# Attention with a gated MLP on one core: k and v loads of later heads moved, the last burst reordered, its last pieces stored from where they are made

## The chip, the cores and the metric

One core of one Trainium2 chip. The metric is the device time of one execution in microseconds (us), as a median over executions. Most questions here are about one or two microseconds in 544, so each result comes with the range of its executions, and comparisons use ratios with a 95% interval. A profiled execution is one of these; its span (first to last instruction) is some 1.8 us shorter than its device time.

All outputs are right.

## The reference, cut to what matters

```python
xn = layernorm(x)                              # x: 2048 x 448
q = (xn @ wq)                                  # 16 heads of 256
k, v = k_cache[last 512], v_cache[last 512]    # 8 heads, each used by two q heads
s = (softmax(q @ k.T / 16) @ v) @ wo           # 2048 x 448
g = silu((gelu(xn @ w_gate) * (xn @ w_up)) @ w_down)
return x + s * g
```

## The kernel before

The kernel is one static program: operations are listed in order, and semaphore waits follow from the buffers that they read and write. The first 145 us make the layer norm and the gates g. The gates go to DRAM (`g_all`) and come back in tiles. Then 64 "heads" follow: 4 chunks of 512 queries by 16 heads. For a head, `s_mm` makes scores and exponentials p; two DMA transposes (`pT<-pn`) turn p for four tiles; `pv`, two heads later (LAG), multiplies by v. Every eight heads a query group makes q for the next eight. After each chunk, a "burst" multiplies o with wo: seven products of halves and sums in place of eight (a Strassen-like scheme), combined on VectorE (DVE).

k and v of the 8 key heads are loaded partly late, because their room is used by temporaries of the gates before. The places of the temporaries of the last two chunks of gates are set here:

```python
a_v, a_th = b_va[3].lo, at2 + 3 * TD
dn[2] = places(2, [(2, a_v), (1, a_v + SD), (0, b_pT[2][0].lo)],
               [a_v + 2 * SD, b_pT[2][0].lo, b_pT[2][0].lo + CD], [a_th])
dn[3] = places(3, [], [a_v + 2 * SD, a_v + SD, a_v + SD + CD], [a_th])
```

The loads stand in the main loop, between the query pairs of the group at head 4 (m == Q0) and the group at head 12 (m == Q0 + QS); `gates3` computes the last gates and stores them:

```python
if m == Q0 and p < 3:
    K.reuse(b_kT[2:6] + b_va[3:4] if p == 0 else b_kT[6:] + b_va[4:] if p == 2 else [])
    for k in ((2, 3, 4, 5), (), (6,))[p]:
        load_k(k)
    if p == 0:
        load_v(3)
    if p < 2:
        gates3(2 * p)
        gates3(2 * p + 1)
    else:
        load_v(4)
        load_v(5)
        K.reuse([b for y in b_xr for b in y])
        for t in range(NG2):
            load_g2(t)
        for t in range(NXR):
            dma("pool", xr[:, t, :], x_view[:, t, :], (), b_xr[t])
if m == Q0 + QS and p == 0:
    load_k(7)
    load_v(6)
    load_v(7)
```

The loads of g and x at the end of that stretch are issued by GpSimd and feed the first burst, over 70 us later. `load_g2(t)` reads `g_all`, so it waits for the gates' stores.

In the burst, B1 is the bank (in the last burst: two banks, one for each half of 128 rows) of the first product, B6, B7, B5, B3 those of the products with sums, B4 that of product 3:

```python
def product(j, b, lhs, hs, first, reads, ts=(0, 1)):
    mms([(bank[b][:, t * N2:(t + 1) * N2], lhs(h)[:, t * P:(t + 1) * P], wt[:, WAT[j], h, :],
          first and h == hs[0] and t == ts[0], False) for h in hs for t in ts],
        reads + [b_wt[j][i] for i in sorted({h * NB // Hq for h in hs})], (b_ps[b],))

def first_two(j, hs, first):
    A1 = A(j, 0)
    for ts in (((0,), (1,)) if last else ((0, 1),)):
        product(j, B1[ts[0]], A1, hs, first, bA(j, hs), ts)
```

```python
for n in range(3):
    sums(n)
first_two(0, allh[:Hq - LAG], True)
if last:
    pv(late.pop(0))
    pv(late.pop(0))
first_two(0, allh[Hq - LAG:], False)
if last:
    K.reuse(b_lastt + b_lastg)
    for i in range(2):
        dma("pool", lastt[:, i, :], g2d[NT - 2 + i], (b_g2d[NT - 2 + i],), (b_lastg[i],))
    dma("pool", lastt[:, 2, :], x_view[:, NT - 1, :], (), b_lastt)
    for t in range(2):
        cs = slice(t * N2, (t + 1) * N2)
        act(U2[:, cs], bank[B1[t]][:, cs], ACT.Copy, (b_ps[B1[t]],), bU2, scale=F)
else:
    act(U2, bank[B1[0]][:, 0:D], ACT.Copy, (b_ps[B1[0]],), bU2, scale=F)
    product(3, B4, A(1, 1), allh, True, bA(1, allh))
for n in range(Hq // HB):
    hs = allh[n * HB:(n + 1) * HB]
    for j, i, b in ((5, 2, B6), (6, 3, B7), (4, 0, B5), (2, 1, B3)):
        product(j, b, lambda h, n=n, i=i: sr[n % 3][:, i, h % HB, :], hs, n == 0, [b_sr[n % 3][i]])
    if n == 0:
        sums(3)
if last:
    product(3, B4, A(1, 1), allh, True, bA(1, allh))
first_two(1, allh, False)
plus(U2, bU2, B6, U2, bU2)
plus(U3, bU3, B7, U2, bU2)
if not last:
    part(1, 0, B4, U3, bU3)
part(1, 1, B5, U3, bU3)
plus(U2, bU2, B5, U2, bU2)
part(0, 1, B3, U2, bU2)
ends((2, 1), (3, 1), (0, 1), (1, 1))
if last:
    part(1, 0, B4, U3, bU3)
    ends((2, 0), (3, 0))
for t in range(2):
    first_part(t)
    ends((t, 0))
```

After the last matmul, `first_part` copies half a bank to SBUF on ScalarE (ACT), and `burst_end` multiplies by g, adds x and stores:

```python
def burst_end(t, ns=(0, 1)):

    t4 = t % 4
    x, bx = (xr[:, t % NXR, :], b_xr[t % NXR]) if t < NT - 1 else (lastt[:, 2, :], b_lastt)
    g, bg = (g2[:, t % NG2, :], b_g2[t % NG2]) if t < NT - 2 else (lastt[:, t % 2, :], b_lastg[t % 2])
    cs = slice(ns[0] * N2, ns[-1] * N2 + N2)
    bx, by = [[b[n] for n in ns] for b in (bx, b_xs[t4])]
    add("dve", xs[:, t4, cs], xs[:, t4, cs], g[:, cs], by + [bg], by, ALU.mult)
    if t + NG2 < NT - 2:
        load_g2(t + NG2)
    add("dve", x[:, cs], xs[:, t4, cs], x[:, cs], by + bx, bx)
    dma("sp" if t >= NT - 4 else "pool", out_view[:, t, cs], x[:, cs], bx, ())
    if t + NXR < NT - 1:
        dma("pool", xr[:, t % NXR, :], x_view[:, t + NXR, :], (), b_xr[t % NXR])
```

The softmax here doesn't subtract the row's maximum and nothing guards it: scores larger than these inputs give would overflow.

## Time and profile before

| | before |
|---|---|
| device time, 3 runs | 543.7 us median (543.29 to 545.11) |
| profiled span | 542.4 us |
| TensorE busy | 536.5 us, 99% |
| TensorE waits after the start | head 4's p (pT) 0.9 us, o of the last chunk (oTh) 0.3 us |
| from the last ACT copy's start to the end | 3.23 us |

How to read the lines in this document. In the list of waits, a line says which engine at which source line waited for what, the sum in us, how often, and the longest. In a timeline, a line gives start, duration, engine, source line, operation, output<-input, shapes, how many instructions it lumps together, and in brackets the idle time before it and what ended it. SPq and POOLq are the queues of the SyncE and GpSimd engines as issuers of DMA. The source line is nearly always that of a helper (one line for all matmuls, one for all copies on ACT, and so on), so tiles tell the operations apart: pT<-pn the transposes of p, g<-g_all and xr<-in_A_x_dram the GpSimd loads, bank<-kT,qT scores, bank<-pT,va p times v, bank<-wt,oTh and bank<-wt,sr the products of the burst.

The *lost start* before a matmul is the distance between its start and the start of the one before, less that one's columns / 2.4 ns and 2.5 ns. The *landing* of a DMA is the moment when the last of its 16 parts has counted its semaphore up.

### The profile page before, as it was taken

The page shows a single profiled execution, that of the slowest core. Times are in us where ns is not written, and L with a number is a line of the kernel's source. Part 1 is how long each engine was busy: PE and PEld are TensorE (multiplying, and loading weights), DVE is VectorE, ACT ScalarE, POOL GpSimd, SP SyncE. Part 2 cuts the span into 40 slices and gives each one's busy share as a digit, 9 for nine tenths or more (in the row PEclk, how much of TensorE's full clock was granted, in tenths as well). Part 3 has the DMA queues.
Part 4 walks back from the last instruction along what each step waited for, and adds up shares of the span by engine and source line. Part 5 has one row for each costly group of instructions (what it writes and reads, how often), then busy time and mean ns, then how long its engine had stood idle before and what let it go on. Part 6 is the DMA issues. An engine that isn't in the chain of part 4 may idle for free.

```text
span 542.4 us, 10788 instructions
## 1 busy us (share of the span) xinstructions
PE 536.5 (99%) x4106; PEld 305.8 (56%) x4106; DVE 375.8 (69%) x823; ACT 313.8 (58%) x784; POOL 39.6 (7%) x78
## 2 busy tenths in 40 slices
PE   8999999999999999999999999999999999999997
PEld 5554457449644444984444469544444984444487
DVE  6673885799767757934875786367568934776875
ACT  5433854873667858216875860488488116877720
POOL 1130400000001000003001000120100003001010
PEclk9999999999999999999999999999999999999999
DMA  9569261931499848302781670076457502863621
GB/s 292 125 184 132 47 140 42 272 92 43 114 194 190 156 113 149 70 1 70 166 152 47 153 139 1 18 150 146 94 102 156 64 1 78 160 151 85 155 48 34
DMA packets 171459, 61.36 MB, mean 113 GB/s; under 512 B 154960, under 2 KB 168272, under 8 KB 171408
## 3 DMA queue, kind: packets, MB, share of 16 engines
q1 hardware_dynamic: 167632, 51.39, 45.0%
q0 software_dynamic: 3008, 8.72, 6.7%
q8 instruction: 32, 0.52, 0.4%
q10 hardware_dynamic: 768, 0.57, 0.3%
q14 instruction: 19, 0.16, 0.1%
HBM read 19.76 MB, written 3.67 MB: 43 GB/s over the span
## 4 chain that ended last, share of the span: by engine, by line
PE 93%; ACT 2%; DVE 2%; DMA 2%; issue 1%; ACTq 0%
PE bank L391 92%; ACT p L843 2%; DMA pT<-pn 2%; DVE pn L850 1%; PE bank L508 1%; DVE rden L847 0%; ACT qT L382 0%; PE bank L489 0%; ACT oTh L382 0%; ACT xnT L382 0%; DVE xnT L385 0%; DVE xr L385 0%; DVE gl L421 0%; DVE epst L422 0%; ACTq L155 0%
## 5 line engine op out<-in xcount | busy, mean ns | idle before, releaser
L843 ACT ACTIVATE p<-bank 128x512 f32<-128x512 f32 x256 | 150.5, 596 | 28.8 <-DVE pn L850 26.0
L391 PE MATMUL bank<-pT,va 128*128 128x512 bf16 x512 | 120.9, 379 | 1.0 <-DMA pT<-pn 0.9
L391 PE MATMUL bank<-kT,qT 128*128 128x512 bf16 x512 | 121.0, 379 | 0.0
L850 DVE TENSOR_SCALAR pn<-p,rden 128x512 bf16<-128x512 f32 x256 | 113.1, 484 | 10.2 <-DMA pT<-pn 6.0
L391 PE MATMUL bank<-xnT,wq 64*128 64x512 bf16 x768 | 94.9, 376 | 0.0
L391 PEld LDWEIGHTS bank<-pT,va 128*128 128x128 bf16 x512 | 49.7, 98 | 62.0 <-DMA pT<-pn 3.4
L391 PEld LDWEIGHTS bank<-kT,qT 128*128 128x128 bf16 x512 | 49.4, 98 | 61.7 <-issue 3.4
L391 PE MATMUL bank<-xnT,wgu 64*128 64x512 bf16 (+2 forms) x768 | 83.8, 350 | 0.2
L382 ACT ACTIVATE qT<-bank 128x512 bf16<-128x512 f32 x76 | 44.1, 596 | 51.7 <-PE bank L391 50.1
L828 DVE CAST qT<-bank 128x512 bf16<-128x512 f32 x52 | 34.9, 690 | 49.6 <-PE bank L391 49.6
L391 PEld LDWEIGHTS bank<-xnT,wq 64*128 64x128 bf16 x768 | 36.7, 94 | 46.3 <-ACT p L843 2.1
L391 PEld LDWEIGHTS bank<-xnT,wgu 64*128 64x128 bf16 x768 | 36.8, 94 | 37.2 <-issue 0.6
L847 DVE RECIPROCAL rden<-rsum 128x2 f32<-128x2 f32 x128 | 21.2, 165 | 46.0 <-ACT p L843 45.8
L843 ACT ACTIVATION_READ_ACCUMULATOR p<-bank 128x1 f32 x256 | 51.6, 202 | 0.0
L391 PE MATMUL bank<-wt,sr 128*128 128x224 f16 x512 | 49.7, 259 | 0.0
L382 ACT ACTIVATE gl<-bank 128x512 bf16<-128x512 f32 x56 | 33.1, 596 | 28.5 <-PE bank L391 26.1
L391 PEld LDWEIGHTS bank<-wt,sr 128*128 128x128 f16 x512 | 49.1, 98 | 0.0
L382 ACT ACTIVATE xnT<-bank 128x224 bf16<-128x224 f32 (+2 forms) x12 | 4.4, 398 | 71.6 <-PE bank L391 70.9
L868 DVE TENSOR_SCALAR oTh<-bank 128x512 f16<-128x512 f32 x62 | 42.4, 684 | 0.0
L382 ACT ACTIVATE oTh<-bank 128x512 f16<-128x512 f32 x66 | 38.9, 589 | 4.7 <-PE bank L391 4.7
L391 PE MATMUL bank<-wt,oTh 128*128 128x224 f16 x384 | 38.3, 259 | 0.3 <-ACT oTh L382 0.3
L391 PEld LDWEIGHTS bank<-wt,oTh 128*128 128x128 f16 x384 | 36.7, 98 | 1.8 <-ACT oTh L382 1.1
(80 smaller groups left out, 408.2 us busy)
## 6 DMA issues: line engine op xcount, KB each, us to landing
wtb<-in_A_wo_dram POOLq DMA_DIRECT2D x4, 896.0 KB, 10.9
wq<-in_A_wq_dram SPq DMA_DIRECT2D x2, 1536.0 KB, 7.9
va<-in_A_v_cache_dram SPq DMA_DIRECT2D x8, 256.0 KB, 3.9
pT<-pn SPq DMA_TRANSPOSE x128, 2.8
xr<-in_A_x_dram POOLq DMA_DIRECT2D x15, 112.0 KB, 2.3
wd<-in_B_w_down_dram SPq DMA_DIRECT2D x1, 1568.0 KB, 8.5
g<-g_all POOLq DMA_DIRECT2D x14, 112.0 KB, 2.3
out_dram<-xr POOLq DMA_DIRECT2D x12, 112.0 KB, 2.1
```

Of the source, the lines that this page charges most:

```text
L382: K.op("act", lambda e, o=o, i=i: e.activation(o, i, func, scale=scale), reads, writes)
L391: ins = e.matmul(o, lhsT=l, rhs=r, start=st, stop=sp, skip_group_check=True)
L508: ins = e.matmul(bank[b][:, 0:w], lhsT=gl[:, 0, 0:P], rhs=gl[:, 0, 0:w], start=True, stop=True)
L828: K.op("dve", lambda v, s=s, b=b: v.tensor_copy(qT[:, s, 1, :], bank[b + 1]), (b_ps[b + 1],), (b_qT[s][1],))
L843: K.op("act", lambda e, b=b, r=r, z=z: e.activation(p32[:, z, :], bank[b], ACT.Exp, scale=att_scale, accum_out=rsum[:, r:r + 1]), (b_ps[b] ...
L847: K.op("dve", lambda e, r=r: e.reciprocal(rden[:, r - 1:r + 1], rsum[:, r - 1:r + 1]), b_rsum[r - 1:r + 1], b_rden[r - 1:r + 1])
L850: K.op("dve", lambda e, r=r - 1 + t, z=(n - 1 + t) % NP32, y=y, t=t: e.tensor_scalar(pn[:, y, t, :], p32[:, z, :], rden[:, r:r + 1], None, ...
L868: K.op("dve", lambda v, i=i, b=b: v.tensor_scalar(oTh[:, i, :], bank[b], WS, None, op0=ALU.mult), (b_ps[b],), (b_oT[i],))
```

## The change

Intent: take load off the DMA ahead of head 4's p; give head 15's o time before it is needed; shorten the chain after the last matmul. Four parts:

1. *k and v.* At head 4: k2 to k5, v3, v4 in one go, ahead of the last gates. At head 12: k6, k7, v5, v6, v7. The gates' temporaries move up to the end of v's room to make way for v4. The GpSimd loads of g and x are written in the second group now, but their issue waits only for data, so they still go out with the gates' stores.
2. *Late heads.* In the last burst, heads 14 and 15 enter the first product behind the first 32 matmuls on sums.
3. *Narrow pieces.* The second half of that product gets two banks and is made in two pieces of 112 columns.
4. *Last pieces.* `last_end` multiplies straight from the bank and stores from xs (xnT in the profile), with no ACT copy. (In the other bursts two ACT copies become one of 448 columns.)

```diff
-        dn[2] = places(2, ..., [a_v + 2 * SD, ...], [a_th])
-        dn[3] = places(3, [], [a_v + 2 * SD, a_v + SD, a_v + SD + CD], [a_th])
+        dn[2] = places(2, ..., [b_va[-1].hi - CD, ...], [a_th])
+        dn[3] = places(3, [], [b_va[-1].hi - i * CD for i in (1, 2, 3)], [a_th])
...
+        def last_end(t, c0, c1, i, b_i, f):
+            ...
+            K.op("dve", lambda e: e.scalar_tensor_tensor(
+                out=xs[:, t4, c0:c1], in0=i, scalar=f, in1=g[:, c0:c1], op0=ALU.mult, op1=ALU.mult), ...)
+            add("dve", xs[:, t4, c0:c1], xs[:, t4, c0:c1], x[:, c0:c1], by + bx, by)
+            dma("sp", out_view[:, t, c0:c1], xs[:, t4, c0:c1], by, ())
...
-                B1, B6, B7, (B5, B3, B4) = AB[:2], AB[2], AB[3], BB[:3]
+                B1, B6, (B5, B3, B4, B7) = AB[:3], AB[3], BB
...
+            pieces = [(B1[0], (0,), 0, N2), (B1[1], (1,), 0, N4), (B1[2], (1,), N4, N2)] if last else [...]
...
-            first_two(0, allh[:Hq - LAG], True)
+            for hs in (allh[:Hq - 2 * LAG], allh[Hq - 2 * LAG:Hq - LAG]):
+                first_two(0, hs, hs[0] == 0)
             if last:
                 pv(late.pop(0))
                 pv(late.pop(0))
-            first_two(0, allh[Hq - LAG:], False)
...
                 if n == 0:
                     sums(3)
+                    if last:
+                        first_two(0, allh[Hq - LAG:], False)
...
-            for t in range(2):
-                first_part(t)
-                ends((t, 0))
+                for b, (t,), c0, c1 in pieces:
+                    last_end(c * 4 + t, c0, c1, bank[b][:, t * N2 + c0:t * N2 + c1], b_ps[b], F)
...
-                    if m == Q0 and p < 3:
-                        ... k2 to k5, v3 | gates | k6, v4, v5, g, x
+                    if m == Q0 and p == 0:
+                        K.reuse(b_kT[2:6] + b_va[3:5])
+                        ... k2 to k5, v3, v4
                     ...
                     if m == Q0 + QS and p == 0:
-                        load_k(7); load_v(6); load_v(7)
+                        ... k6, k7, v5, v6, v7, g, x
```

## The prediction

> **What bounds the kernel now.** I read the page's first part, then who waits for whom, then stretches of the timeline around each wait of the TensorE, then its end.
>
> ```profile
> PE 536.5 (99%) x4106; PEld 305.8 (56%) x4106; DVE 375.8 (69%) x823; ACT 313.8 (58%) x784; POOL 39.6 (7%) x78
> ...
> PE bank L508 <- DVE epst L422: 1.2, 1, 1.2
> PE bank L391 <- DMA pT<-pn: 0.9, 1, 0.9
> PE bank L391 <- ACT oTh L382: 0.3, 1, 0.3
> ```
>
> The TensorE is busy 99% of a span of 542.4 us and waits three times; the first is the start, which the change leaves alone. No other engine is over 69%. The granted clock is at its top in all 40 slices. So time can come from three places only: the two remaining waits, the number and width of matmuls, and the tail after the last matmul.
>
> A wait in this view understates its loss, because a matmul's modelled end lies some 0.16 us behind the point at which the next could start. I therefore take starts. A head's eight 512-wide matmuls start every 215.5 ns, 1.725 us per eight.
>
> ```profile
> 167.29 1.89 PE L391 MATMUL bank<-kT,qT 128*128 128x512 bf16 x8
> 170.08 1.90 PE L391 MATMUL bank<-pT,va 128*128 128x512 bf16 x8 [0.91 <-DMA pT<-pn]
> ...
> 511.77 1.89 PE L391 MATMUL bank<-pT,va 128*128 128x512 bf16 x8
> 513.99 0.75 PE L391 MATMUL bank<-wt,oTh 128*128 128x224 f16 x6 [0.33 <-ACT oTh L382]
> ```
>
> First pair: the second eight could have started at 167.29 + 1.725 = 169.01; they started at 170.08: 1.07 us lost. Second pair: 511.77 + 1.725 = 513.49 against 513.99: 0.50 us lost.
>
> The queue shows why the first one waits:
>
> ```profile
> 158.52 1.89 SPq L379 DMA_TRANSPOSE kT<-in_A_k_cache_dram  x1
> 160.45 1.14 SPq L376 DMA_DIRECT2D va<-in_A_v_cache_dram  x2
> 163.51 9.66 SPq L379 DMA_TRANSPOSE pT<-pn  x5
> ...
> 161.74 1.10 POOL L376 DMA_DIRECT2D g<-g_all  x2 [94.00 <-DMA g_all<-g]
> 162.83 1.83 POOL L376 DMA_DIRECT2D xr<-in_A_x_dram  x3
> ```
>
> One k head, two v heads and five tiles of 112 KB are issued just ahead of the first transposes of p for head 4. The chain of waits has such a transpose at 4.82 us (165.21 to 170.04), while the median of all 128 is 2.8 us on the page.
>
> The end:
>
> ```profile
> 538.64 1.86 SPq L376 DMA_DIRECT2D out_dram<-xr  x2
> 539.17 0.36 ACT L382 ACTIVATE xnT<-bank 128x224 bf16<-128x224 f32 x1 [1.18 <-PE bank L391]
> 539.56 0.28 DVE L385 TENSOR_TENSOR xnT<-xnT,g 128x224 bf16<-128x224 bf16 x1 [0.95 <-ACT xnT L382]
> 539.87 0.27 DVE L385 TENSOR_TENSOR xr<-xnT,xr 128x224 bf16<-128x224 bf16 x1
> ```
>
> Last matmul, copy on ACT, two operations on DVE (done at 540.14), store. From the copy's start to the span's end are 542.4 - 539.17 = 3.23 us.
>
> **What the Trainium skill says.** "TensorE: Matmul & The Clock Gate", section "Wait — 56ns, not 53.3ns?": warm matmuls start N / 2.4 GHz + about 2.5 ns apart. The trace agrees: 215.5 ns at 512 columns, 95.9 ns at 224 (128 matmuls from wt, sr in 12.43 us). For 112 columns that makes 49 ns, an estimate. The same page, "Back-to-back issue gap", gives about 81 ns per matmul at N = 128 for streams that load weights each time, and "LDWEIGHTS" says a load scales with its columns; the trace has no full-height matmul under 224 columns, but its transposes (64 rows, 128 weight columns, 64 moving) start in pairs 29 ns apart, so a load need not cost more than that. "DMA: Bandwidth & Descriptors", "Anatomy of one DMA": about 2 us are fixed and mostly the write's receipt; here the last store takes from 540.18 to the end at 542.4, so halving its bytes should win nothing.
>
> **The change part by part.**
>
> *k and v.* The instruction order shows: in the query group at head 4, k2 to k5 and now v3 and v4 go first, then the gates' stores; k6 and v5 leave this stretch for the query group at head 12, which gets k6, k7, v5, v6, v7. New places for the gates' temporaries free v4 early. So 512 KB (k6, v5) vanish from the 5 us ahead of head 4's p, and v4 (256 KB) goes earlier. The GpSimd loads do not move: they wait only for the stores of g, which come some 0.6 us later behind v4. At 220 GB/s (the windows view between 164 and 170 us) 512 KB are 2.4 us of backlog; the wait was 1.07. I take all of it as gone, and 1.0 for the mean, since 560 KB of GpSimd loads still overlap. In the later group, k6 is needed when the group ends: it runs from 189.1 to 198.3 (9.2 us), and before, k7 was issued there at 191.5 and had landed 3.3 us after. k6 takes that place and lands some 3.5 us ahead. v5 is third in the row, behind 2.6 us of issue for k6 and k7 (1.3 each), so it lands by about 198 and is needed 1.7 us after the group's end. No new wait: 0. Sum -1.0.
>
> *Late heads behind the first sums.* The first product now starts with heads 0 to 11, whose o has long been evacuated, so the 0.50 us goes. Heads 12 and 13 follow 2.3 us later, then p times v of heads 14 and 15, then 32 matmuls on sums, then heads 14 and 15 in the product. Two prices. Bank 3 of the second set now takes sum product 7: it is free only when ACT has copied head 15's second half, which in the trace starts 0.20 us after the last p-v matmul could be followed (520.39 against 520.19) and takes 0.60, with 0.06 to the TensorE: 0.86 us, while eight matmuls of 95.9 ns cover 0.77: +0.1. And the p-v of heads 14 and 15 comes 0.4 us earlier, while head 15's second transpose landed at 518.4, just in time (the weight load at 518.45 waited for it). That landing was late by chance of place: issued 514.59, others of this stage need 2.8 us, and a 16 KB fetch of instructions at 515.4 held one DMA engine 1.2 us. With more and shorter matmuls ahead, that fetch moves 0.6 us earlier. I give it +0.1. Sum -0.50 + 0.10 + 0.10 = -0.3.
>
> *Narrow pieces.* 32 matmuls of 224 columns become 64 of 112: 64 x 49 - 32 x 95.9 ns = +0.07 us. Other 112-wide effects: none.
>
> *Last pieces.* In the tail, the ACT copy (0.36), its handover, a 0.28 multiply and a 0.27 add become one scalar_tensor_tensor from the bank and one add, 112 wide. Durations: that operation takes 0.62 at 448 columns and DVE copies from a bank 0.69 at 512, so about 1 ns a column; at 112 an estimate of 0.28, at 224 of 0.40. Adds take 0.27 at 224 and 0.39 at 448, so 0.21 at 112. Before: from 539.17 to 540.14 is 0.97. After: 0.28 + 0.03 + 0.21 = 0.52. The DVE is free in time: its work on the other three quarters ends at 537.84, then piece one (0.40 + 0.27) to about 538.55, piece two (0.28 + 0.21) to 539.06, before the last bank is done at 539.2. The store keeps its time. -0.45.
>
> *Other bursts.* Two ACT copies become one of 448: off the path, 0.
>
> Sum: -1.0 - 0.3 + 0.07 - 0.45 = -1.7 us, 543.7 - 1.7 = 542.0.
>
> **The rivals.**
>
> 1. *The backlog only moves.* The wait for p at head 4 stays in part because the GpSimd loads and the gates' stores alone are enough, or a new one stands at head 12 where five loads are now issued in a row. For it: the DMA is 90% busy or more in nearly all slices between 155 and 166. Against it: in the later stretch (189 to 198) its share is 0.65 and the demand there is five loads in 9 us. It would leave 542.6 to 543.1.
> 2. *Weight loads bind the narrow matmuls.* If the 81 ns of the skill held, 64 x (81 - 49) = 2.0 us are added and the change would come out at about 544. Against it the transposes at 29 ns a pair; and each weight load in the trace starts at the start of the matmul before it and takes a fixed 98 ns whatever that one's width, so this is a latency and not an occupancy, which I cannot prove for full height.
> 3. *The handover wait reappears.* Head 15's transpose lands where it did: the 0.50 us are lost again just ahead of its p-v. 542.4.
>
> **Range and chances.** Weighed: the main line with 60%, rival 1 in some part 20%, rival 2 in some part 10%, rival 3 20%, with some overlap. The three runs of before spread over 1.8 us, their two lower ones over 0.4. I predict 542.0, range 541.2 to 543.2. 2% is 10.9 us, and all that can be removed is the two waits and part of a 3.2 us tail: faster by over 2% 0.005, within 2% 0.99, slower 0.005.
>
> **What would show it.** In the waits of the TensorE the line for pT<-pn should be gone or under 0.2, and so the one for oTh; if a wait on pT<-pn stands near 198 or 516, rivals 1 or 3. The 112-wide matmuls should start 49 ns apart, with a busy mean near 212 ns (259 less 112 / 2.4); 80 apart is rival 2. From the last matmul's end to the span's end should be 2.75 us in place of 3.2. The prediction is wrong if the TensorE's starts are no closer anywhere, or if a store of 224-byte rows takes longer than one of 448-byte rows.

## The result, and the profile after

| | before | after |
|---|---|---|
| device time, 6 runs each on the same chip | 544.32 us (542.98 to 545.11) | 543.99 us (543.34 to 545.16) |
| ratio, after over before | | 0.9998 (0.9979 to 1.0017) |
| profiled span | 542.4 us | 541.5 us |
| lost start at head 4 | 1.07 us | 1.19 us |
| lost start ahead of the burst's first product or in it | 0.49 + 0.05 us | 0 + 0.09 us |
| from the last evacuation's start to the end | 3.23 us | 3.10 us |

A ratio is the mean time of one kernel's runs over that of the other's of the same rounds, so it is not quite the ratio of the medians. The predicted time was 542.0 us with a range of 541.2 to 543.2; the median of 543.99 lies above it. No change was shown.

The list of waits of the changed kernel (the first line is in the opening, before 10 us, and so is a third of 0.4 us that is left out here):

```profile
PE bank L509 <- DVE epst L423: 1.2, 1, 1.2
PE bank L392 <- DMA pT<-pn: 1.0, 1, 1.0
```

The wait for oTh has gone. The wait for pT, which was to go, is still there and as long as it was. The chain of waits names the same transpose, 5.29 us from issue to landing, and nothing but matmuls from there to the last one:

```profile
164.73 5.29 DMA pT<-pn
170.02 0.05 issue
170.07 368.31 PE bank L392 x2592
```

The timeline of the TensorE around it, then that of the two issuing queues ahead of it:

```profile
167.15 1.89 PE L392 MATMUL bank<-kT,qT 128*128 128x512 bf16 x8
170.07 1.90 PE L392 MATMUL bank<-pT,va 128*128 128x512 bf16 x8 [1.03 <-DMA pT<-pn]
```

```profile
155.70 1.41 SPq L377 DMA_DIRECT2D va<-in_A_v_cache_dram  x2
157.15 0.98 SPq L377 DMA_DIRECT2D g_all<-g  x2
158.19 2.27 SPq L377 DMA_DIRECT2D g_all<-g2w  x2
163.28 5.53 SPq L380 DMA_TRANSPOSE pT<-pn  x3
...
162.59 1.32 POOL L377 DMA_DIRECT2D g<-g_all  x2 [94.99 <-DVE rden L848]
163.90 1.59 POOL L377 DMA_DIRECT2D xr<-in_A_x_dram  x3
```

The SyncE queue did what was intended: no k or v goes out in the 6 us before 163.28; v3 and v4 went at 155.7 and 156.6. But the five GpSimd loads stand exactly on the transposes: issued from 162.59 to 164.96, landed from 165.17 to 169.05, with the two transposes issued at 163.28 and 164.73 landing at 168.49 and 170.02.

The handover to the last burst, in the timeline of the TensorE, has no wait and the intended new order:

```profile
511.37 1.89 PE L392 MATMUL bank<-pT,va 128*128 128x512 bf16 x8
513.10 2.88 PE L392 MATMUL bank<-wt,oTh 128*128 128x224 f16 x42
515.82 3.62 PE L392 MATMUL bank<-pT,va 128*128 128x512 bf16 x16
519.27 3.33 PE L392 MATMUL bank<-wt,sr 128*128 128x224 f16 x32
522.43 0.55 PE L392 MATMUL bank<-wt,oTh 128*128 128x224 f16 x6
```

And the end. In the timeline, DVE's last operations and the last stores; in the view of the DMA from 536.5 us on, the column after the size is the median from issue to landing:

```profile
537.67 2.14 SPq L377 DMA_DIRECT2D out_dram<-xnT  x3
...
538.40 0.28 DVE L898 SCALAR_TENSOR_TENSOR xnT<-bank,g 128x112 bf16<-128x112 f32 x1 [0.26 <-PE bank L392]
538.71 0.22 DVE L386 TENSOR_TENSOR xnT<-xnT,xr 128x112 bf16<-128x112 bf16 x1
```

```profile
q8 instruction: 1, 0.02, 0.9%
...
out_dram<-lastt SPq DMA_DIRECT2D x1, 56.0 KB, 2.9
out_dram<-xnT SPq DMA_DIRECT2D x1, 56.0 KB, 2.5
out_dram<-xnT SPq DMA_DIRECT2D x2, 28.0 KB, 1.9
```

The DVE did the work in 0.53 us as predicted (0.52), done at 538.93. The span ends 2.57 us later all the same, where it ended 2.26 us after DVE's last operation before (540.14 to 542.4). (The span is printed to 0.1 us, so such differences are good to 0.05; the unrounded records give 3.15 us from the last evacuation's start to the end, and 3.20 before.) The three stores ahead of the last were slower, 2.3 to 2.9 us to landing. The last landed in 1.57 us, but it was issued at 539.38, 0.45 us after its data were there. Among them lies one packet of the queue named "instruction". The page of the whole span has 33 of them, and the page of before 32:

```profile
q8 instruction: 33, 0.54, 0.4%
```

```profile
q8 instruction: 32, 0.52, 0.4%
```

0.54 MB by 33 is 16 KB each. I take them for fetches of the TensorE's instructions: there is about one for 256 of its matmuls and weight loads (2 x 4138 / 33 = 251). That reading is put to the test below. In this trace the 33rd runs from 537.8 for 1.18 us.

*The sum of the two traces.* The matmuls start 0.14 us earlier from the opening on (a marker at 48 us), head 4 loses 0.12 more, two small waits of before (0.14 at 275 us and 0.22 at 363 us) are absent, the handover gains 0.45, the narrow pieces cost 0.07, the tail gains 0.13: -0.14 + 0.12 - 0.36 - 0.45 + 0.07 - 0.13 = -0.89, against 541.5 - 542.4 = -0.9. So nothing is missing in this pair; but more than half of it (the opening, the two small waits) is scatter and not the change, and the timed runs show nearly nothing of it.

### The profile page after: what moved, and what is told of

Same layout as the page of the kernel before. It is cut to its first block, busy times and chain, and to the rows that moved or that the text cites. A ratio compares the mean times of both kernels' runs of the same rounds, so it can differ in the third digit from the quotient of the medians.

```text
span 541.5 us, 10848 instructions
## 1 busy us (share of the span) xinstructions
PE 535.7 (99%) x4138; PEld 306.3 (57%) x4138; DVE 376.3 (69%) x825; ACT 313.4 (58%) x780; POOL 39.5 (7%) x78
## 4 chain that ended last, share of the span: by engine, by line
PE 97%; DMA 1%; DVE 0%; issue 0%; ACT 0%; ACTq 0%
PE bank L392 97%; DMA pT<-pn 1%; DMA x<-in_A_x_dram 0%; DVE stats L439 0%; PE bank L490 0%; DVE xn L465 0%; DVE mv L442 0%; ACT p L844 0%; PE bank L509 0%; DVE xnT L898 0%; DVE xnT L386 0%; DVE rstd L459 0%; ACTq L155 0%
## 5 line engine op out<-in xcount | busy, mean ns | idle before, releaser
L392 PE MATMUL bank<-wt,oTh 128*128 128x224 f16 (+1 forms) x416 | 38.4, 252 | 0.0
L377 POOL DMA_DIRECT2D g<-g_all x14 | 7.8, 556 | 379.9 <-DVE xnT L386 285.0
```

Source lines behind the costliest of these rows:

```text
L377: K.op(q, lambda e, o=o, i=i: e.dma_start(o, i), reads, writes, dma=True)
L392: ins = e.matmul(o, lhsT=l, rhs=r, start=st, stop=sp, skip_group_check=True)
```

## The experiments

The theories, as the traces and the first runs suggested them: (T1) the GpSimd loads alone delay head 4's p; (T2) 64 more TensorE instructions move and add instruction fetches, which fall on the last stores. Rivals: it is scatter; the gates' stores or a fetch near 158 us delay p; the narrow matmuls or narrow stores themselves cost the tail.

A summary first, since each experiment feeds it. All are single traces, one for each label. The 0.09 us ahead of product 7, the same in every trace with the change's banks, is not in the column of the handover, nor are losses under 0.1 us.

| trace | head 4 lost start, us | in the handover, us | other |
|---|---|---|---|
| before | 1.07 | 0.49 + 0.05 | 0.14 at 275, 0.22 at 363 |
| before_again | 2.29 | 0.49 | 1.15 at 365, slow clock at 172 |
| burst_only (old k and v) | 2.03 | 1.35 | 0.10 at 208 |
| after | 1.19 | 0 | |
| after_again | 1.63 | 1.96 | 0.30 at 403 |
| after_third | 0.94 | 0 | |
| kv_only | 0.74 | 0.49 | |
| no_split | 1.16 | 0.22 | 0.18 at 275, 0.17 at 363 |
| no_split_dummy | 0.62 | 0 | |
| dummy_20 | 0.49 | 0.13 | |
| split_few_warm | 0.79 | 1.22 | |
| shift_fetch | 1.05 | 0 | 0.57, 0.39, 0.34, 0.29 at 266, 365, 379, 422 |
| late_gx | 0 | 0 | 1.08 at 210 |
| before_late_gx (old k and v) | 0 | 0.49 | 0.34 at 206 |
| best | 0 | 0 | 0.51 at 210 |
| best_two | 0 | 0 | 0.16 at 186 |

In some of these traces about 25 matmul records are missing, which shows as gaps of exactly one matmul (216 ns) and as small waits for qT in the list of waits; they are left out.

### after_again

No edit: the changed kernel once more, on the chip of the next three.

> The changed kernel itself, unedited: a second trace and five more timed rounds. If the first trace was typical: a wait of 0.8 to 1.2 us on p's transpose at 168 to 170 us, a 33rd fetch of the TensorE's instructions at about 538 us, the last store issued about 0.45 us after its data was ready, ratio to before 0.997 to 1.001. If the wait at head 4 was a matter of that one run, it is under 0.3 us here and the span is 540.3 us.

Measured: 544.15 us (543.15 to 546.48), ratio to before 0.999 (0.996 to 1.002). Its traced execution was the longest of the six (546.48, span 544.7), where the first traced one was the shortest. The list of waits has 3.3 us in two waits for pT, where the first trace had one of 1.0 us; the second is in the handover:

```profile
516.94 1.90 PE L392 MATMUL bank<-pT,va 128*128 128x512 bf16 x8
520.64 1.90 PE L392 MATMUL bank<-pT,va 128*128 128x512 bf16 x8 [1.80 <-DMA pT<-pn]
```

The oTh wait is gone here as well, but head 15's own p came late: its second transpose was issued at 516.15 and landed at 520.59, 4.44 us, where the first trace had 2.83. What follows: one trace of a kernel shows a mechanism and not its mean. The rival in which the handover wait reappears for p does happen, in some executions.

### late_gx

The five loads of g and x are held back until the TensorE has finished the scores of heads 13 to 17.

```diff
-                        for t in range(NG2):
-                            load_g2(t)
-                        for t in range(NXR):
-                            dma("pool", xr[:, t, :], x_view[:, t, :], (), b_xr[t])
...
             s_mm(m)
+            if Hq - 3 <= m < Hq + 2:
+                pe = [last TensorE operation]
+                t = m - (Hq - 3)
+                ... load_g2(t) for t < 2, else x tile t - 2, after=pe
```

> The changed kernel with the five GpSimd loads of g and x (560 KB) held back, one each behind the scores of heads 13 to 17. Theory (these loads, which start only when the gates' stores have landed, share the DMA engines with the two transposes of head 4's p and delay them): transposes of head 4 take under 3.5 us in place of 5.2 and 5.3, the wait at 168.7 us is under 0.2, span about 540.3, ratio 0.995 to 0.998. Rival (the loads of k and v and the gates' stores on the queue of the SyncE are the backlog, or the fetch of instructions at 158 us): the transposes stay over 4.5 us, the wait stays over 0.8, ratio near 1.

Measured: 543.03 us (542.58 to 544.36), ratio to before 0.9965 (0.9938 to 0.9992). The wait at head 4 is gone altogether; the timeline of the TensorE runs through:

```profile
167.95 1.89 PE L392 MATMUL bank<-kT,qT 128*128 128x512 bf16 x8
169.67 1.89 PE L392 MATMUL bank<-pT,va 128*128 128x512 bf16 x8
```

The stretches of 4 us say why. Columns: window and length, busy time of PE, weight loads, DVE, ACT, POOL with counts, granted clock, DMA share, GB/s. First the changed kernel, then late_gx:

```profile
164.00:168.00 4.00, 4.00 (x20) 1.78 (x19) 2.51 (x7) 3.25 (x11) 1.49 (x3) 1.00 1.02 201
```

```profile
164.00:168.00 4.00, 4.00 (x21) 1.81 (x19) 2.83 (x9) 3.51 (x12) 0.00 (x0) 1.00 0.58 131
```

With the GpSimd loads the DMA engines are full; without them they are 58% busy, and head 4's two transposes take 2.72 and 2.77 us in place of 5.21 and 5.29. T1 holds. The price is that the first two of the held-back loads meet another head's transposes, at 210 us, together with an instruction fetch at 206.6: these transposes took 5.14 and 5.12 us, and 1.08 us were lost. That is a matter of where the loads go. The traced span of 542.6 us missed the expected 540.3 for this wait and for an opening 0.8 us longer than in the change's trace.

### no_split

Two pieces of 224 columns in place of 224 + 112 + 112; the rest of the change stays.

```diff
-            pieces = [(B1[0], (0,), 0, N2), (B1[1], (1,), 0, N4), (B1[2], (1,), N4, N2)] if last else [...]
+            pieces = [(B1[0], (0,), 0, N2), (B1[1], (1,), 0, N2)] if last else [...]
```

> The changed kernel with the last product in two pieces of 224 columns in place of three (no 112-wide matmuls; 32 matmuls fewer), stores as in the change. Theory (the 64 further instructions of the narrow pieces call for one more 16 KB fetch that falls among the last stores and costs about 0.45 us there): 32 fetches in place of 33, every store lands within 1.6 us of its issue, the last store is issued at once; the tail's two operations cost 0.18 more; span 541.1 to 541.3. Rival (no fetch effect, the narrow pieces win what they were meant to): span 541.7 to 541.9.

Measured: 543.07 us (542.5 to 544.05), ratio to before 0.9964 (0.9935 to 0.9993). 32 fetches again, none near the end. Its span ends 2.97 us after the start of the last evacuation (538.83 to 541.8), against 3.10, 3.20 and 3.15 in the three traces of the change, though its last DVE operations are longer (0.39 + 0.28 in place of 0.28 + 0.22). Undoing a part whose purpose was to shorten the tail shortened it a little. The span itself, 541.8 us, lay in the range that I had given to the rival (541.7 to 541.9) and not in that of the theory (541.1 to 541.3); the three small waits of this trace in the table, 0.57 us together, make up that difference, so the tail and not the span decides here.

### best

late_gx and no_split together, and the banks that the code calls B7 and B4 exchanged, so that B7 gets a bank that is free early. (The text counts these products in another way; the banks meant are these two.)

```diff
-                B1, B6, (B5, B3, B4, B7) = AB[:3], AB[3], BB
+                B1, B6, (B5, B3, B7, B4) = AB[:3], AB[3], BB
```

> Late GpSimd loads, two pieces of 224, and the banks of products 7 and 3 swapped so that product 7 doesn't wait for the evacuation of head 15's second half (0.09 us in the changed kernel's trace). Theory: no wait at head 4 (1.19), none in the first sums (0.09), no 33rd fetch (0.35 net): span 539.8 to 540.2, ratio to before 0.993 to 0.997. Rival as in the runs on single parts: 541 or more.

Measured: 542.57 us (541.9 to 542.85), ratio to before 0.9954 (0.9929 to 0.998). No lost start at head 4 nor in the burst; the 0.09 us on bank B7 that the traces with the change's banks have is gone; 0.51 is left at 210 us. With that and an opening 0.5 us longer than in the change's trace, the span of 541.1 us missed the expected 539.8 to 540.2.

### kv_only

Before, with part 1 of the change alone.

```diff
+                       [b_va[-1].hi - CD, b_pT[2][0].lo, b_pT[2][0].lo + CD], [a_th])
+        dn[3] = places(3, [], [b_va[-1].hi - i * CD for i in (1, 2, 3)], [a_th])
...
+                    if m == Q0 and p == 0:
+                        ... k2 to k5, v3, v4
...
+                    if m == Q0 + QS and p == 0:
+                        ... k6, k7, v5, v6, v7, g, x
 (nothing in the burst)
```

> The kernel before with the change's placement of k and v alone (and the places of the gates' temporaries that go with it); last burst as before. Theory (the GpSimd loads of g and x delay head 4's p, so moving k6 and v5 away wins nothing): the wait at 168 us stays between 0.8 and 1.7 us, transposes of head 4 over 5 us, 32 fetches; handover wait of 0.5 us and the tail as before; ratio to before 0.998 to 1.002. Rival (the placement works and the GpSimd loads are not to blame): wait under 0.3.

Measured: 543.99 us (543.2 to 545.4), ratio to before 0.9979 (0.9936 to 1.0022): not told apart from before. Lost start at head 4 0.74; the transposes there took 4.83 and 4.80 us, so the GpSimd loads still sit on them. Both are a little under what the theory had asked for (0.8 and 5 us), and far over the rival's 0.3.

### burst_only

The change without part 1.

```diff
-        dn[3] = places(3, [], [b_va[-1].hi - i * CD for i in (1, 2, 3)], [a_th])
+        dn[3] = places(3, [], [a_v + 2 * SD, a_v + SD, a_v + SD + CD], [a_th])
...
-                        ... k2 to k5, v3, v4
+                        ... k2 to k5, v3 | gates | k6, v4, v5, g, x
 (the burst as in the change)
```

> The changed kernel with k and v placed as in the kernel before: last burst and last pieces alone. Theory: the wait at head 4 is about 1.1 us as before; the 0.5 us at the handover is gone unless a fetch of instructions strikes head 15's transpose; 33 fetches, the last among the stores; span about 0.7 under that of before, ratio 0.997 to 1.001.

Measured: 544.17 us (542.76 to 546.13), ratio to before 0.9974 (0.9934 to 1.0015): no difference shown either. In its list of waits pT stands twice:

```profile
PE bank L392 <- DMA pT<-pn: 3.1, 2, 1.9
```

2.03 us of lost start at head 4 and 1.35 in the handover. The tail is the longest of all: 3.55 us from the last evacuation's start, with the 33rd fetch at 540.2. The span of 544.3 us is 1.9 over that of before, where 0.7 under it was expected. So the burst's parts bring their own costs without the moved loads.

### before_again

No edit: the kernel before.

> The kernel before, unedited, for a second trace of it: how much of the run-to-run spread of 2 us is waits. If the waits of the first trace are typical: 0.9 to 1.3 us lost at 168 us, 0.5 at the handover to the last burst; ratio 1.000 within 0.002.

Measured: 544.77 us (543.44 to 547.95), ratio 0.9996 (0.9952 to 1.004). The other eleven executions of before on this chip went from 543.66 to 549.73. The traced one was the longest of its six, and shows what makes an execution of before long: 2.29 us of lost start at head 4 in place of 1.07. In the timeline of the TensorE, and then in a stretch (columns as above):

```profile
171.26 2.95 PE L391 MATMUL bank<-pT,va 128*128 128x512 bf16 x8 [2.12 <-DMA pT<-pn]
```

```profile
171.90:175.40 3.50, 3.50 (x10) 1.25 (x9) 2.61 (x7) 1.65 (x6) 0.00 (x0) 0.51 0.66 150
```

After the wait the granted clock was 0.51 over these 3.5 us, with eight matmul starts 427 ns apart, which lost another 1.7 us. So the first trace of before, on which the prediction's sum stood, was one of the good ones.

The timed executions show the same thing. 3.4 us at half clock in 546 us lower the mean granted clock by 0.003. Of the 56 executions of before in the result and in these batches, ten have a mean clock of 0.993 to 0.997, and they are the ten longest (546.67 to 549.73 us). None of the 69 executions of the other kernels has one under 0.999, not even the 39 with the new places of k and v and the GpSimd loads still on p. So part 1, with its shorter wait at head 4, may have spared the kernel these executions. Only this count says so: burst_only, with the old places, has none among its six either, and none of before's six in the result was of this kind.

### no_split_dummy

no_split with 32 tiny TensorE instructions (32 matmuls of 8 columns and their weight loads) into an already emptied bank, just ahead of product 3. They add as many instructions as the narrow pieces did, without narrow matmuls or stores.

```diff
             if last:
+                mms([(bank[AB[2]][:, 0:8], ident[:, :], ident[:, 0:8], True, True) for _ in range(32)],
+                    [b_ident], (b_ps[AB[2]],))
                 product(3, B4, A(1, 1), allh, True, bA(1, allh))
```

> The two-piece kernel with 32 small matmuls (8 columns, onto an unused bank) ahead of the last products: the instruction count of the changed kernel without its narrow pieces. Theory (the 33rd fetch of instructions, not the width of the stores, delays the last stores): 33 fetches, one of the last three stores takes over 2 us or is issued late; end of the span 1.2 to 2 us after that of the two-piece kernel (about 1.0 for the small matmuls, 0.2 to 1 for the fetch). Rival (224-byte rows made the stores slow): every store lands within 1.6 us.

Measured: 543.93 us (543.21 to 544.88), ratio 0.9971 (0.9933 to 1.001). The 33rd fetch came, as T2 says it must, but at 536.4, earlier than I had reckoned, and met the stores before the last ones: 1.75, 1.81 and 1.63 us to landing where 1.5 to 1.6 is usual. I had expected over 2 us. The tail was 2.90 us. So this shows that instructions of any kind call the fetch, and that a fetch lengthens stores by some tenths; it does not show a longer end.

### before_late_gx

Before, with the held-back loads of late_gx alone.

> The kernel before with nothing changed but the GpSimd loads of g and x held back, one each behind the scores of heads 13 to 17; k and v where they were. Theory (these loads are most of what delays head 4's p, the later k and v the rest): the wait at 168 us falls from 1.1 to 2.3 to under 0.4 us, transposes of head 4 take 2.8 to 3.8 us; a new wait of 0.5 to 1.1 near 209 us where a load and a fetch of instructions meet. Rival (k6, v4, v5 on the SyncE's queue are the main thing): the wait stays over 0.8.

Measured: 543.17 us (542.5 to 544.16), ratio 0.9976 (0.9948 to 1.0004). Here k6, v4 and v5 are still in their old place, landing at 163.1 to 165.1, and head 4 loses nothing: its transposes took 2.77 and 3.09 us. In the timeline of the TensorE:

```profile
167.33 1.89 PE L391 MATMUL bank<-kT,qT 128*128 128x512 bf16 x8
169.06 1.89 PE L391 MATMUL bank<-pT,va 128*128 128x512 bf16 x8
```

0.34 is lost at 206 us. This is the clearest verdict on part 1: k and v in front of p do not make it late by themselves. Moving g and x is enough; moving k and v is not.

### best_two

best with the held-back loads placed elsewhere: the two of g after the scores of heads 7 and 8, one of x after those of head 11, the other two of x with the query group at head 12.

```diff
+            if m in (7, 8, 11):
+                pe = [last TensorE operation]
+                ... load_g2(m - 7) after pe for 7 and 8, x tile 0 for 11
...
                     if m == Q0 + QS and p == 0:
+                        pe = [last TensorE operation]
+                        for t in (1, 2):
+                            dma("pool", xr[:, t, :], x_view[:, t, :], (), b_xr[t], pe)
```

> As the best so far, with the five GpSimd loads at heads 7, 8 and 11 and two in the query group at head 12, away from the fetch of instructions near 206 us that met them. Theory: no wait at 168 nor at 209 us, all waits of the TensorE on p under 0.3 in sum, span 540.0 to 540.8, ratio to before 0.992 to 0.996. Rival (wherever 560 KB go, they cost 0.5 us): a wait of 0.4 to 1 us at 175 to 200 us, span 541.

Measured: 541.97 us (541.61 to 542.11), ratio to before 0.9952 (0.9922 to 0.9982), and the narrowest range of all. Its list of waits has the start and nothing else:

```profile
PE bank L509 <- DVE epst L423: 1.2, 1, 1.2
```

The last evacuation in its timeline:

```profile
537.22 0.39 DVE L898 SCALAR_TENSOR_TENSOR xnT<-bank,g 128x224 bf16<-128x224 f32 x1 [0.72 <-PE bank L392]
```

540.1 - 537.22 = 2.88 us of tail. This version beats before: the mean is 0.48% under it, some 2.6 us, or 2.1 without the two executions of before at a lower clock. It shared no rounds with the change, but its longest execution (542.11) lies under the shortest of the change (543.04). Its range of half a microsecond suggests what the others' scatter was made of. Transposes of p over 4 us are still in its trace; none of them makes the TensorE wait more than 0.16 us.

### split_few_warm

The change with 8 warm-up matmuls taken away at the start (16 instructions with their weight loads), which brings the count of instructions down below the 33rd fetch. It is slower at the start on purpose.

```diff
-        warm(9, 2, QC)
+        warm(1, 2, QC)
```

> The changed kernel with 8 of the 9 wide warm-up matmuls at the start left out: 16 instructions of the TensorE fewer, so that the 33rd fetch should not be called for or only after the end; three narrow pieces as in the change. The start is slower on purpose, only the tail counts. Theory: 32 fetches, all three last stores land within 1.65 us of issue and the last is issued within 0.1 us of its data. Rival (narrow stores are slow by themselves): last store late by 0.4 us as before.

Measured: one execution, 545.87 us, slow for the start as intended; only the end is read. 32 fetches, three narrow pieces. The timeline of the end:

```profile
540.55 1.62 SPq L377 DMA_DIRECT2D out_dram<-xnT  x3
...
541.28 0.27 DVE L898 SCALAR_TENSOR_TENSOR xnT<-bank,g 128x112 bf16<-128x112 f32 x1 [0.26 <-PE bank L392]
541.59 0.22 DVE L386 TENSOR_TENSOR xnT<-xnT,xr 128x112 bf16<-128x112 bf16 x1
```

The three stores are issued within 1.62 us (2.14 in the change's trace), they land after 1.46 to 1.53 us, and the span ends 543.9 - 541.28 = 2.62 us after the last evacuation's start. With the same narrow pieces the change had 3.10. So the narrow pieces do shorten the tail, by 0.6 us from before's 3.23, once no fetch falls on it. The handover lost 1.22 us in this trace.

### dummy_20

no_split with 20 of the dummy matmuls, meant to bring the 33rd fetch later, onto the last stores.

```diff
-  for _ in range(32)
+  for _ in range(20)
```

> The two-piece kernel with 20 small matmuls in place of 32, so that the 33rd fetch falls some 1.2 us nearer to the end, among the last stores, with 448-byte rows. Theory: one of the last two stores takes over 1.9 us or is issued over 0.2 us late. Rival: all land within 1.65 us.

Measured: one execution, 543.2 us. No 33rd fetch came at all (32 in the page). The tail is 2.93 us, as without dummies. The run decides nothing on the question that it was made for; it only bounds the count at which the fetch comes: not at 4126 matmuls (nor at 4130 in split_few_warm), but at 4138.

### shift_fetch

The change with more, shorter warm-up matmuls, so that every later fetch comes some 5 us earlier.

```diff
-        warm(9, 2, QC)
+        warm(6, 2, QC)
+        warm(51, 2, 8)
```

> The changed kernel with three of the nine wide warm-up matmuls replaced by 51 of 8 columns: 96 instructions of the TensorE more ahead of everything, about the same time at the start, so every later fetch of instructions comes 48 matmuls earlier (about 5 us at head 4, 10 us at the handover, 3 us at the end). Theory (fetches that hit the transposes of p and the stores make the waits at the handover and at the end): no wait over 0.2 us on p between 514 and 519 us, last store issued within 0.1 us of its data and the end 2.2 to 2.3 us behind the last matmul; at head 4 the GpSimd loads alone still leave 0.3 to 0.8. Ratio to before 0.995 to 0.998. Rival (the waits are chance or lie in the transposes themselves): a handover wait over 0.2 or a late last store again.

Measured: 544.45 us (543.36 to 545.85), ratio 0.9996 (0.9975 to 1.0018). Three readings. First, the tail: the 33rd fetch came at 536.2, ahead of the last stores, which landed in 1.45 to 1.55 us, and the span ended 2.68 us after the last evacuation's start (541.42 to 544.1). Second, head 4: the fetch that stood at 158 us came at 153.3, the stores of the gates lost the straggling sixteenth part that they have in other traces, and p was late all the same (5.65 and 5.03 us, 1.05 lost). So that fetch is not needed for head 4's wait. Third, the handover: with its fetch at 507.2 all of the last four transposes took 2.73 to 2.79 us, and nothing was lost.

But the kernel is not faster: four other transposes were late, at 266, 365, 379 and 422 us, 1.59 us in all. I expected the shift to be free, and it was not. Its trace says what they met: the transposes behind those at 266, 379 and 422 us overlap fetches at 262.7, 375.3 and 419.0, and those at 365 us met no fetch but DMAs of GpSimd, an x load from 361.9 to 366.3 among them.

### after_third

No edit: the change once more, a single execution on the last chip.

> The changed kernel once more, for a third trace: wait at head 4 between 0.5 and 1.7 us; handover wait either 0 or 1.2 to 2.0; 33rd fetch within the last stores, end 2.7 to 3.2 us behind the last matmul.

Measured: 543.04 us, span 541.3. 0.94 lost at head 4, nothing in the handover, tail 3.15 us with the 33rd fetch at 537.5.

## Why the prediction was wrong, point by point

*What failed first: "I take all of it as gone, and 1.0 for the mean".* Head 4's wait did not go. In nine traces with the new places of k and v and the GpSimd loads where they were, it is 0.49 to 1.63 us, 0.96 in the mean. The working had counted the 512 KB of k6 and v5 as the backlog, divided by 220 GB/s, and compared that with the wait. It treated the transfers as one queue in which less ahead means earlier. But the last of k, v and the gates' stores had landed at 162.97 in the changed kernel, before p was even issued at 163.28. What was in flight with p were the 560 KB of GpSimd loads, issued within 2.4 us around it. The text named them and left 0.07 us for them. The prediction's first rival, that "the GpSimd loads and the gates' stores alone are enough", was right in its first half: late_gx and before_late_gx take those loads away and leave the stores, and the wait is 0 in both, and in best and best_two. Its figure for the time, 542.6 to 543.1, was still too low, since the other steps failed too. (The DMA share that it cites as 90% or more in nearly all slices is so in 30 of the 40 between 155 and 165 us.)

Part 1 was not worth nothing. The three traces with old k and v have 1.07, 2.29 and 2.03 us, 1.80 in the mean, so the saving may be about 0.8 us. That rests on three traces; timed, kv_only against before gives 0.9979 with an interval of 0.9936 to 1.0022, too wide to show it.

*"Last pieces ... -0.45": mis-sized, to about 0.* The arithmetic on DVE was right to 0.01 us. "The store keeps its time" was wrong. The term missed that the 64 extra TensorE instructions call for one more 16 KB fetch, and that the count puts it some 4 us before the kernel's end (3.4 to 4.1), in all five traces of this tail with the fetch placed so. The prediction had itself put head 15's late landing in the handover down to a fetch, and did not ask where the added one would fall. From the start of the last evacuation to the end: before 3.23, 3.23, 3.19 and 3.17 us in four traces; change 3.10, 3.20, 3.15, with burst_only 3.55 and late_gx 3.35; predicted 2.78. Two runs removed the collision, by fewer instructions ahead and by more, and had 2.62 and 2.68. So the idea was worth 0.55 to 0.6 us, more than predicted, and the narrow pieces themselves bought the event that ate it. Two pieces without it stand at 2.88 to 2.97. That the fetch is the cause is shown by those two runs and by the lengthened stores; that a fetch alone, without narrow pieces, lengthens the end was to be shown by the dummies and was not, since it fell elsewhere.

*Handover, "-0.50 + 0.10 + 0.10 = -0.3": right in kind, too large in the mean.* The oTh wait of 0.49 is gone in every trace of the new order, and the bank of product 7 costs 0.09 in every trace with the change's banks, 0.10 predicted. The term for head 15's transpose was 0.1. Its traces with three pieces give 0, 1.96, 0, 1.35, 0, 0 and 1.22: 0.65 in the mean, which with the 0.09 is more than the 0.49 + 0.05 that before lost. The third rival had this as 0.50 at most, "just ahead of its p-v", which is where it stands. With two pieces five traces give 0.07 in the mean. Both orders put 2.7 us of matmuls ahead of that p-v. An instruction fetch lies at 512.0 to 514.7 in the three-piece traces, and shift_fetch, which moved it, had no wait, but late_gx had the fetch at 513.4 and no wait, so its presence alone does not decide it. The traces show what the three that waited have in common. The transposes just ahead of head 15's second one met the fetch, and that one went out 0.80 to 0.92 us after its p was made (0.03 to 0.67 in the other nine traces of the new order). Then three GpSimd loads of the last tiles (`lastt`, 336 KB, first used 13 us or more after they land) were issued 0.80 to 0.93 us behind it (1.03 to 1.70 in the others), and it took 3.76 to 4.44 us (2.79 to 3.02). That is head 4's pattern again, but no run moved these loads, so it is not shown. Whether three pieces have to do with it is open.

*Narrow pieces, +0.07: right.* The 112-wide matmuls start 49 ns apart (49 at the 10th and 50 at the 90th percentile), so the second rival, weight loads that bind, is dead.

*No new wait at head 12: right.* None of the traces with the new places has one within that group: k6 and v5 were in time. *Other bursts, 0: right.*

*The base.* The sum was taken from 543.7, the median of three executions. The medians of before in later batches were 544.32, 545.04, 544.26, 543.68 and 543.94, and the trace from which the waits were read had an unusually short wait at head 4. Put together from the means of the traces, the change is worth -0.84 (head 4) + 0.20 (handover, 0.65 + 0.09 - 0.54) + 0.07 + 0.06 (tail, 3.27 over five traces less 3.21 over four) = about -0.5 us, and 544.32 - 0.5 = 543.8 against 543.99 measured. This is an estimate from few traces, and the timed ratios cannot confirm a half microsecond; but it needs no further cause.

*What lengthens a transpose.* All 16 traces together have 2048 transposes of p. Of the 1483 with neither an instruction fetch nor a GpSimd DMA in flight in the 2.7 us after their issue, the median is 2.73 us and none took over 4. With a fetch alone it is 4.22 us (300, of which 183 took over 4); with a GpSimd DMA alone 3.03 us (251, of which 37 took over 4). All 229 over 4 us met one or the other. Moving the fetch moved the late ones: with it at 507.2 in shift_fetch the transposes issued at 505.4 and 506.8 took 4.24 and 3.69 us and the later ones 2.72 to 2.79; in the change, with it at 512.0, those issued at 510.7 and 512.8 took 4.64 and 3.61. Most cost nothing, since the TensorE had work.

*Still open.* Why head 4's wait ranges from 0.49 to 1.63 us between executions of nearly the same program. It goes with the length of the fetch near 158 us (1.13 to 1.20 us in four traces with 0.49 to 0.79 lost, 1.59 to 1.68 in four with 0.94 to 1.63), but shift_fetch, without a fetch there, lost 1.05. And whether the `lastt` loads make p of head 15 late.

## What to carry to other kernels

When a transfer is late, list what was in flight during it on every queue, and take away each suspect alone before rebuilding the order: here the loads that nobody needed for 70 us were the cause, and holding them back with a wait on an unrelated engine was worth more than the whole change. More instructions are not free even where their time is: they shift and add instruction fetches, and in these traces transfers that met one landed later, a transpose of p by 1.5 us in the median, so look at where these fall relative to the last stores and to the transfers that something waits for. And read waits from several traces of the same kernel before giving one of them a value to the tenth of a microsecond.

## What the Trainium skill lacked or had wrong

- "Runtime: NRT & Kernel Launch", section "Instruction fetch mechanics", says that instructions are refilled by DMA in 16 KiB blocks of 256 instructions, and that crossing a boundary is "mostly hidden". The traces agree with the blocks (33 for 8276 matmuls and weight loads, 0.54 MB) and show the TensorE not waiting for them. The page lacks the other side: a fetch takes 0.9 to 2.8 us (median 1.1), and data transfers under way at the time land late. Transposes of p took 4.22 us in the median with a fetch on them and 2.73 without. In the change's tail, three stores took 2.3 to 2.9 us where they took 1.5 without it, the last was issued 0.45 us late, and the span's end moved by about 0.5 us (3.10 against 2.62 and 2.68).
- "TensorE: Matmul & The Clock Gate", section "Back-to-back issue gap", gives about 81 ns per matmul at 128 columns for streams with a weight load each. Measured: 49 ns at 112 columns, with a weight load for each, at full height and the warm clock. At 512 columns the same sentence gives about 131 ns, and the starts here are 215.5 ns apart. The formula of the section "Wait — 56ns, not 53.3ns?" holds for both (112 / 2.4 + 2.5 = 49.2; 215.8).
- The same page, section "What's actually happening", has the clock fall to half after at least one idle window of about 3.4 us. In before_again the TensorE stood idle for 2.12 us only, and the trace's clock record has it at half from 171.96 to 175.37, beginning 0.7 us after the matmuls had resumed; the 3.4 us ahead of the fall held 1.3 us of matmuls. Waits with 1.80 us idle (after_again, whose next eight matmuls still took 1.90 us) and 1.9 us idle (burst_only) were not followed by a fall.
- "DMA: Bandwidth & Descriptors", section "Anatomy of one DMA", puts the fixed part at about 2.0 us for transfers from GpSimd. The prediction used it for stores from SyncE, which the section is not about; its 2.2 us from 540.18 to 542.4 are 1.53 to the landing and 0.7 after it. These stores, 28 and 56 KB, land 1.45 to 1.6 us after issue when no fetch is in flight, and halving the bytes took off less than 0.1 us (1.45 to 1.48 against 1.53).
- No page that I found gives the time of a transpose by DMA within SBUF when plain loads from another queue share the engines: 2.7 us alone, 4.5 to 6.8 us (the first two of head 4) with 560 KB of loads from GpSimd issued within some 2.4 us.
